# Starting every weight slab on a whole 256 bytes in a convolution and gated-FFN kernel on TensorE

## The chip, the core and the metric

The kernel runs on one core of one Trainium2 chip. The metric is device time in microseconds (us) of one execution. The kernel before takes 1324.0 us, the median of three runs (1322.94 to 1324.1).

The engines carry the names of the profile: PE is TensorE's matmuls, PEld its weight loads (they run beside the matmuls), DVE is VectorE, ACT is ScalarE, POOL is GpSimd, SP is SyncE, which here only issues DMAs. SBUF is the on-chip memory that the tiles lie in: 128 partitions, and in each a line of bytes. An address below is a byte in that line, the same in every partition.

## The reference

The first half is a short dynamic convolution: for each token and each of 8 heads, a softmax over 7 weights mixes the token with its 6 predecessors. The second is a gated feed-forward layer.

```python
w = exp(weight_gen - max);  w = w / (sum(w) + 1e-9)        # (4, 4096, 8, 7)
out[b,s,h,:] = sum_k w[b,s,h,k] * x_pad[b, s+k, h, :]       # x: (4, 4096, 192)
x = out.reshape(16384, 192)
gate = 1 / (1 + exp(-(x @ w_gate)))                         # w_gate: (192, 1536)
val  = x @ w_val                                            # w_val:  (192, 1536)
y    = (gate * val) @ w_out                                 # w_out:  (1536, 192)
```

## The kernel before

**Work and tiles.** The 16384 tokens are cut into 33 blocks: two of 256 tokens, then 31 of 512. The 1536 hidden features are cut into 12 slices of 128, numbered f = 0 to 11. One block with one slice is a *period*; there are 33 x 12 = 396 of them, and TensorE runs them one after the other.

**Weights.** Each slice f has one weight *slab* that stays in SBUF for the whole run: a tile of 128 partitions x 1152 fp32 numbers, 4608 bytes in each partition. It holds the gate, value and output weights of the slice twice, as a high and a low part, so that products of two parts each give more precision (`convert`; the split is made once, at the start). The slab is first the landing place of the raw weights (`raw`), and becomes `W` in place. Slabs 10 and 11 are used once more before that, for selection matrices (`sel_h`, `sel_t`), and so they are the first two that are allocated.

**Matmuls.** All matmuls of the periods come from line 911, in `emit`. Each uses 64 of TensorE's 128 rows: its weights are 64 partitions x 128 columns of a slab, its moving operand 64 partitions x 512 tokens (256 in the first two blocks) of `A`, `As` or `T` (the convolved tokens, in two parts) or of `hh` and `hl` (gate times value, in two parts). Two such matmuls, one on the lower and one on the upper 64 rows, run side by side; the text calls this a *pair*, and the time from the start of one matmul to the start of the next on the same 64 rows the *pitch*. A period has 14 pairs: 18 matmuls with slab f (gate and value), 10 with the slab of an earlier period, three periods back from block 4 on (the output product). In a block, therefore, the periods of f = 10 and 11 load 18 of their 28 weights from slab 10 or 11, those of f = 1 and 2 load 10 of 28 from them, and f = 0, which lies between, none; f = 3 to 9 use slabs 0 to 9 alone.

**The other engines.** DVE convolves the next block (lines 688 and 734), and for each period multiplies gate and value (L970) and forms `hl` (L976). ACT makes the sigmoid (L967) and `hh` (L973). After the last slice of a block, ACT moves the head of the output out of PSUM (L1023); by the three-period delay this stands right behind the period of f = 2. POOL does nothing but a 1 x 1 memset of the tile `seen` (L906), which passes the turn when one output bank goes from the upper to the lower rows. `w2` holds the softmax of the very first block (128 partitions x 7 x 32 numbers); it is used at the start only. `eye` is a small matrix for `convert`.

**Order.** A planner in the program (`Plan.order`) simulates the engines with fixed costs and so decides the order of all instructions. No address of a tile enters into it.

**Addresses.** Tiles of the pool `sb` are laid out in the order in which they are first asked for, each beginning on a multiple of 32 bytes. All tiles from `w0` to `cu1` end on a multiple of 256 bytes. Then come `w2` (896 bytes), `eye` (1024), slabs 11 and 10, `seen` (4 bytes, so 32 with the gap), and slabs 0 to 9. The moving operands `A`, `As`, `T`, `hh` and `hl` all begin on a multiple of 256; inside a slab every group of 128 columns begins a multiple of 256 bytes behind the slab's start.

Of the kernel before, what the change touches and what calls it, by code (L numbers as in the profile page):

```python
# [9 lines left out]
F32 = mybir.dt.float32  # L10
F32R = mybir.dt.float32r
# [219 lines left out]
def conv_gated_ffn(ctx: ExitStack, tc: tile.TileContext, xt, wg, wcat, outT):  # L231
# [13 lines left out]
    P = 128  # L245
    B, D, SP_ = xt.shape
    NF = wcat.shape[0]
    H, K = 8, 7
# [13 lines left out]
    sb = ctx.enter_context(tc.tile_pool(name="sb", bufs=1))  # L262
# [71 lines left out]
    t = 20.0  # L334
# [248 lines left out]


    CH = blks[0][2] // 8
    w2 = sb.tile([P, K, CH], F32R, name="w2")
    ident = plan.places["ev"][0]["buf"][:, :P]
    eye = sb.tile([P, 2, P], F32R, name="eye")

# [299 lines left out]


    writer = {}
    seen = sb.tile([1, 1], F32, name="seen")
    SYNC = mybir.DependencyInfo(mybir.DependencyClass.Sync, mybir.DependencyReason.DATA)

    def emit(slots):
# [234 lines left out]
```

## Time and profile before

| what | value |
|---|---|
| median of three runs | 1324.0 us (1322.94 to 1324.1) |
| the profiled execution's own time | 1323.46 us |
| its span, first to last instruction | 1321.7 us |
| PE busy | 1294.5 us, 98% |
| PEld busy | 1218.1 us, 92% |
| DVE busy | 1019.4 us, 77% |
| ACT busy | 619.7 us, 47% |
| POOL busy | 136.0 us, 10% |
| granted TensorE clock | 0.999 of full speed |
| chain that ended last: PE | 94% |

Busy time is the time in which an engine ran at least one instruction, so two matmuls side by side count once, and a busy PE is not by itself a PE at its peak. The chain that ended last is followed back from the last instruction, at each step to what released it. PE makes up nearly all of it, and the granted clock is full almost everywhere.

### The profile page before, as it was taken

What the parts mean: (1) busy time and instruction counts of PE and PEld (TensorE: products, weight loads), DVE (VectorE), ACT (ScalarE), POOL (GpSimd) and SP (SyncE); (2) the same over time, 40 slices, a digit from 0 to 9 for tenths busy, and PEclk for the clock granted to TensorE, in tenths of its full rate; (3) what the DMA queues carried; (4) which work ended last, traced back from release to release, by engine and by line L of the source; (5) the groups of instructions that cost most, each with busy time, mean ns of one, the idle gap of its engine ahead of it and who ended that gap; (6) DMA issues with size and microseconds to landing.
All of it is one profiled execution on the core that took longest, in us unless ns stands there. A gap on an engine that the chain in (4) does not pass through costs nothing.

```text
span 1321.7 us, 29878 instructions
## 1 busy us (share of the span) xinstructions
PE 1294.5 (98%) x11196; PEld 1218.1 (92%) x11196; DVE 1019.4 (77%) x1522; ACT 619.7 (47%) x1090; POOL 136.0 (10%) x1517
## 2 busy tenths in 40 slices
PE   5989999999999999999999999999999999999998
PEld 3787888899999999999999998888899999999997
DVE  8989799979998998787766778766688776654443
ACT  5756554454445564444444444444444444444443
POOL 0111101111111111111111111111111111111110
PEclk9999999999999999999999999999999999999999
DMA  8472886459898645534544443544453441011100
GB/s 275 104 161 52 171 181 144 97 129 188 177 187 194 155 105 140 132 99 102 126 99 113 124 120 85 129 107 115 109 132 91 111 116 42 13 37 37 37 13 13
DMA packets 59233, 150.81 MB, mean 114 GB/s; under 512 B 12688, under 2 KB 30992, under 8 KB 59088
## 3 DMA queue, kind: packets, MB, share of 16 engines
q1 hardware_dynamic: 59088, 148.91, 47.1%
q8 instruction: 87, 1.43, 0.5%
q14 instruction: 58, 0.48, 0.1%
HBM read 110.66 MB, written 16.20 MB: 96 GB/s over the span
## 4 chain that ended last, share of the span: by engine, by line
PE 94%; DVE 2%; ACT 1%; issue 1%; DMA 0%; SPq 0%; ACTq 0%; DVEq 0%; POOL 0%; POOLq 0%
PE bank L911 93%; PE bank L448 1%; DVE prod L688 0%; DVE prod L734 0%; DVE sg L970 0%; DMA w<-in_weight_gen 0%; DVE prod L757 0%; PE bank L449 0%; DVE ce L419 0%; DVE hl L976 0%; PE bank L450 0%; DMA out<-osb 0%; DVE cr L432 0%; ACT As L803 0%; DVE acc L688 0%
## 5 line engine op out<-in xcount | busy, mean ns | idle before, releaser
L911 PE MATMUL bank<-hh,W 64*128 64x512 f32 (+1 forms) x2376 | 789.3, 387 | 0.7 <-POOL seen L906 0.3
L911 PE MATMUL bank<-As,W 64*128 64x512 f32 (+1 forms) x2376 | 667.6, 387 | 0.0
L911 PE MATMUL bank<-T,W 64*128 64x512 f32 (+1 forms) x2376 | 661.9, 385 | 0.5 <-ACT T L843 0.4
L911 PE MATMUL bank<-hl,W 64*128 64x512 f32 (+1 forms) x1584 | 607.2, 385 | 3.6 <-DVE hl L976 3.6
L911 PE MATMUL bank<-A,W 64*128 64x512 f32 (+1 forms) x2376 | 496.3, 386 | 1.3 <-DVE A L786 1.3
L973 ACT CAST hh<-sg 128x512 fp32r<-128x512 f32 (+1 forms) x396 | 240.7, 608 | 496.2 <-DVE sg L970 494.1
L911 PEld LDWEIGHTS bank<-hh,W 64*128 64x128 f32 x2376 | 432.9, 184 | 17.2 <-POOL seen L906 2.8
L911 PEld LDWEIGHTS bank<-As,W 64*128 64x128 f32 x2376 | 431.4, 184 | 13.6 <-issue 0.3
L911 PEld LDWEIGHTS bank<-T,W 64*128 64x128 f32 x2376 | 430.2, 184 | 14.2 <-ACT T L843 1.0
L970 DVE TENSOR_TENSOR sg<-bank,sg 128x512 f32<-128x512 f32 (+1 forms) x396 | 265.6, 671 | 187.6 <-PE bank L911 181.9
L976 DVE TENSOR_TENSOR hl<-sg,hh 128x512 fp32r<-128x512 f32 (+1 forms) x396 | 264.9, 669 | 95.0 <-ACT hh L973 92.5
L911 PEld LDWEIGHTS bank<-A,W 64*128 64x128 f32 x2376 | 321.3, 184 | 16.4 <-DVE A L786 1.6
L967 ACT ACTIVATE sg<-bank 128x512 f32<-128x512 f32 (+1 forms) x396 | 231.9, 586 | 170.2 <-PE bank L911 166.9
L911 PEld LDWEIGHTS bank<-hl,W 64*128 64x128 f32 x1584 | 291.3, 184 | 13.8 <-DVE hl L976 5.0
L906 POOL MEMSET seen<- 1x1 f32 x1511 | 135.3, 90 | 1178.9 <-PE bank L911 1174.4
L734 DVE TENSOR_TENSOR prod<-x,wb 128x1024 f32<-128x1024 f32 x126 | 135.8, 1079 | 0.1
L688 DVE TENSOR_TENSOR prod<-prod,prod 128x1024 f32<-128x1024 f32 (+1 forms) x97 | 107.6, 1109 | 0.0
L734 DVE TENSOR_TENSOR prod<-xt,wt 128x1024 f32<-128x1024 f32 (+1 forms) x64 | 68.5, 1071 | 0.8
L688 DVE TENSOR_TENSOR acc<-prod 128x512 f32<-128x512 f32 (+1 forms) x66 | 35.5, 539 | 0.8
L827 DVE TENSOR_TENSOR T<-acc,T 64x256 fp32r<-64x256 f32 (+1 forms) x66 | 26.9, 408 | 1.3 <-ACT T L824 0.3
L824 ACT CAST T<-acc 64x256 fp32r<-64x256 f32 (+1 forms) x66 | 26.2, 397 | 0.8
L1029 DVE TENSOR_TENSOR osb<-bank,ev 64x512 f32<-64x512 f32 (+1 forms) x33 | 21.8, 661 | 5.0 <-ACT ev L1026 4.9
(52 smaller groups left out, 370.7 us busy)
## 6 DMA issues: line engine op xcount, KB each, us to landing
wb<-ws SPq DMA_DIRECT2D x63, 896.0 KB
wt<-ws SPq DMA_DIRECT2D x63, 448.0 KB
As<-A SPq DMA_DIRECT2D x56, 256.0 KB
x<-in_x SPq DMA_DIRECT2D x31, 259.0 KB
out<-osb SPq DMA_DIRECT2D x31, 256.0 KB
T<-T SPq DMA_DIRECT2D x56, 128.0 KB
raw<-in_w SPq DMA_DIRECT2D x12, 576.0 KB
out<-osb SPq DMA_DIRECT2D x33, 128.0 KB
```

The costliest lines, as they stand in the source:

```text
L448: nc.tensor.matmul(dst, eye[:, 0].bitcast(F32), buf[E].bitcast(F32)[:, a:z], start=True, stop=False)
L688: nc.vector.tensor_tensor(out=dst(buf), in0=a(buf), in1=b(buf), op=ALU.add)
L734: nc.vector.tensor_tensor(out=dst.rearrange("p (k i t) -> p k i t", k=z - k, t=M), in0=sliding(buf[X][:, k : k + cols], z - k, [[M, cols / ...
L824: nc.scalar.copy(buf[T][rows, 0, own], buf[ACT_][rows, :M2])
L827: ENG[e].tensor_tensor(out=buf[T][rows, 1, own], in0=buf[ACT_][rows, :M2], in1=buf[T][rows, 0, own].bitcast(F32), op=ALU.subtract,)
L906: turn = nc.gpsimd.memset(seen, 0.0)
L911: ins = nc.tensor.matmul(buf[dst][:, :n], w, m[:, :n], start=start, stop=stop)
L967: nc.scalar.activation(out=buf[k["sg"]][:, :N], in_=buf[k["g"]][:, :N], func=AF.Sigmoid)
L970: nc.vector.tensor_tensor(out=buf[k["sg"]][:, :N], in0=buf[k["v"]][:, :N], in1=buf[k["sg"]][:, :N], op=ALU.mult)
L973: nc.scalar.copy(buf[k["hh"]][:, :N], buf[k["sg"]][:, :N])
L976: ENG[e].tensor_tensor(out=buf[k["hl"]][:, :N], in0=buf[k["sg"]][:, :N], in1=buf[k["hh"]][:, :N].bitcast(F32), op=ALU.subtract)
L1029: nc.vector.tensor_tensor(out=buf[OT][LOW, :N], in0=buf[PT][LOW, :N], in1=buf[EV][LOW, :N], op=ALU.add)
```

## The change

Two small tiles are made larger; only the part that was there before is used.

```diff
-    w2 = sb.tile([P, K, CH], F32R, name="w2")
+    w2 = sb.tile([P, 320], F32R, name="w2")[:, : K * CH].rearrange("p (k t) -> p k t", k=K)
...
-    seen = sb.tile([1, 1], F32, name="seen")
+    seen = sb.tile([1, 128], F32, name="seen")[:, :1]
```

`w2` grows from 896 to 1280 bytes in each partition and `seen` from 4 to 512. What lies behind them in SBUF moves up. The start addresses in the built programs, with the rest by 256 in brackets:

```
tile         before          after
w2           168448 (0)      168448 (0)
eye          169344 (128)    169728 (0)
slab 11      170368 (128)    170752 (0)
slab 10      174976 (128)    175360 (0)
seen         179584 (128)    179968 (0)
slab 0       179616 (160)    180480 (0)
slab 1       184224 (160)    185088 (0)
...
slab 9       221088 (160)    221952 (0)
```

The instructions of all five engines stand in the same order in both programs, with the same shapes; the places in memory alone differ. Before, slabs 10 and 11 begin 128 bytes behind a multiple of 256, and slabs 0 to 9 begin 160 bytes behind one.

## Rows read from the trace of the kernel before

**Rows 1.** The page, busy time of TensorE: us, share, instructions.

```profile
PE 1294.5 (98%) x11196; PEld 1218.1 (92%) x11196; DVE 1019.4 (77%) x1522; ACT 619.7 (47%) x1090; POOL 136.0 (10%) x1517
```

**Rows 2.** Windows: stretch and length, PE, PEld, DVE, ACT, POOL busy; clock; DMA.

```profile
0.00:33.00 33.00, 17.09 (x86) 12.79 (x88) 28.77 (x63) 18.46 (x42) 0.71 (x6) 1.00 0.85 276
33.00:66.00 33.00, 31.59 (x296) 25.44 (x294) 30.91 (x64) 24.24 (x60) 4.09 (x32) 1.00 0.42 104
...
264.00:528.00 264.00, 264.00 (x2267) 261.09 (x2265) 236.80 (x349) 132.27 (x214) 27.70 (x312) 1.00 0.71 160
...
792.00:1056.00 264.00, 264.00 (x2268) 237.41 (x2266) 196.93 (x279) 114.82 (x197) 27.39 (x309) 1.00 0.45 111
...
1280.00:1321.00 41.00, 36.10 (x295) 33.79 (x291) 15.60 (x23) 14.52 (x24) 3.52 (x40) 0.96 0.07 20
```

**Rows 3.** Waits of PE: who waited for whom, us in total, times, longest.

```profile
PE bank L622 <- ACT w L559: 8.2, 1, 8.2
PE bank L449 <- ACT W L439: 5.1, 2, 3.8
PE bank L911 <- DVE hl L976: 3.6, 5, 1.2
```

**Rows 4.** Groups by line and shape, matmuls: count, busy us, mean ns.

```profile
L911 PE MATMUL bank<-hh,W 64*128 64x512 f32 x2232 | 754.8, 392 | 0.3 <-POOL seen L906 0.3
...
L911 PE MATMUL bank<-hl,W 64*128 64x512 f32 x1488 | 581.4, 392 | 0.9 <-DVE hl L976 0.9
```

**Rows 5.** Timeline of PE in a period of f = 6, upper rows: start, us.

```profile
1135.20 0.39 PE L911 MATMUL bank<-hl,W 64*128 64x512 f32 x1
...
1135.43 0.39 PE L911 MATMUL bank<-hh,W 64*128 64x512 f32 x1
...
1135.67 0.40 PE L911 MATMUL bank<-hl,W 64*128 64x512 f32 x1
...
1135.90 0.39 PE L911 MATMUL bank<-A,W 64*128 64x512 f32 x1
```

**Rows 6.** Timeline of ACT, the output's way out of PSUM, two blocks running.

```profile
1124.29 0.59 ACT L1023 COPY osb<-bank 128x512 f32<-128x512 f32 x1
...
1163.48 0.59 ACT L1023 COPY osb<-bank 128x512 f32<-128x512 f32 x1
```

**Rows 7.** Windows over f = 3 to 9, then 10 to 2, twice.

```profile
1124.47:1147.34 22.87, 22.87 (x200) 22.87 (x197) 17.02 (x23) 9.53 (x16) 2.40 (x27) 1.00 0.06 18
1147.34:1163.66 16.32, 16.32 (x144) 16.32 (x142) 11.98 (x19) 7.40 (x14) 1.68 (x19) 1.00 0.20 49
1163.66:1186.54 22.88, 22.88 (x200) 22.88 (x198) 11.20 (x17) 9.53 (x16) 2.40 (x27) 1.00 0.06 19
1186.54:1202.84 16.30, 16.30 (x144) 16.30 (x142) 8.61 (x14) 7.47 (x14) 1.68 (x19) 1.00 0.20 50
```

**Rows 8.** Timeline of PE in a period of f = 10, lower rows, four starts, all from slab 10.

```profile
1148.36 0.39 PE L911 MATMUL bank<-As,W 64*128 64x512 f32 x1
...
1149.06 0.40 PE L911 MATMUL bank<-T,W 64*128 64x512 f32 x1
```

**Rows 9.** Groups of weight loads in one period of f = 10 (1147.34 to 1150.59).

```profile
L911 PEld LDWEIGHTS bank<-As,W 64*128 64x128 f32 x6 | 1.1, 184 | 0.0
...
L911 PEld LDWEIGHTS bank<-A,W 64*128 64x128 f32 x7 | 1.1, 184 | 0.0
```

**Rows 10.** Groups of weight loads over the whole run, output product.

```profile
L911 PEld LDWEIGHTS bank<-hh,W 64*128 64x128 f32 x2376 | 432.9, 184 | 17.2 <-POOL seen L906 2.8 <-issue 1.0
```

**Rows 11.** Timeline of PE in a block of 256 tokens, upper rows, four starts.

```profile
87.40 0.27 PE L911 MATMUL bank<-hh,W 64*128 64x256 f32 x1
...
87.75 0.28 PE L911 MATMUL bank<-hl,W 64*128 64x256 f32 x1
```

**Rows 12.** Windows while raw weights land: slab 9, then slab 10.

```profile
23.07:24.47 1.40, 1.14 (x3) 0.79 (x4) 1.34 (x5) 1.32 (x4) 0.00 (x0) 1.00 1.03 425
24.47:25.87 1.40, 1.40 (x6) 0.92 (x6) 1.40 (x3) 1.34 (x5) 0.00 (x0) 1.00 1.02 421
```

## The prediction

> **What bounds the kernel now.** I read the busy times first: PE is busy for 98% of the span [rows 1]. A busy share alone proves little, so the windows come next. In the first 33 us PE works 17.09 us, and the next 33 us still have a small gap; from then on PE fills its stretches, 264.00 of 264.00 us, at the full granted clock [rows 2]. PE's waits say the same from the other side: the three longest sums, 8.2, 5.1 and 3.6 us, are waits for the first weights and the first values [rows 3]; they are over before the blocks of 512 tokens set in.
>
> So the question is what sets the pace of a matmul, since nobody makes PE wait. The matmuls over 512 tokens are the bulk: the two rows of the output product alone count 2232 and 1488 [rows 4], and by the structure of 14 pairs in each of 31 x 12 periods there are 5208 pairs. On one half of the rows the starts are 1135.20, .43, .67 and .90, so three pitches take 0.70 us, 0.2333 each [rows 5]. The output leaves PSUM once in a block, at 1124.29 and again at 1163.48, 39.19 us apart [rows 6]; divided by 12 x 14 pairs that is 0.2333 again. Thirty-one such blocks make 1215 us of the span of 1321.7. DVE is busy 236.80 us in one stretch of 264 and 196.93 in another, DMA 0.71 and 0.45, and the number of matmuls is 2267 and 2268 [rows 2]. The pace is PE's own: it does not depend on what the other engines or the DMAs do. PEld shows one thing more: it is busy for 261.09 us in the first of these stretches and for 237.41 in the second. Loads on the two halves overlap more in one than in the other, and the pace is the same. How the loads of the two halves lie to each other does not set it.
>
> **The change, part by part.** No instruction is added, removed or moved, on any engine or queue, and no wait. What could cost or gain is the access to the moved tiles: weight loads from the slabs (each of the 11088 matmuls of line 911 has one), the DMAs and the ACT and DVE instructions that fill the slabs at the start, `eye` and `w2` at the start, and the memset of `seen`.
>
> Weight loads. The trace holds its own comparison: slabs 10 and 11 begin at 128 by 256, a multiple of 64 bytes; slabs 0 to 9 begin at 160, which is none. In a period of f = 10, where 18 of 28 loads come from slab 10, the loads take 184 ns in the mean [rows 9]; over the whole run, where ten slabs of twelve lie at 160, they take 184 ns [rows 10]. The load itself does not see the difference.
>
> The pace. Seven periods of f = 3 to 9, all at 160, take 22.87 and 22.88 us, 3.268 each. The five periods f = 10, 11, 0, 1, 2, in which 56 of 140 loads are at 128, take 16.32 and 16.30 us, 3.264 and 3.260 each [rows 7]. (The counts in these rows contain four matmuls that reach over the borders.) Five periods at the other pace would be 16.34, so the mixed ones are 0.02 to 0.04 us shorter in a block, at the limit of what these windows resolve. If aligned loads earn that, it grows with their number; if it belongs to the change of alignment between neighbouring loads, it goes away when all are alike, and 31 blocks cost 0.6 to 1.2 us. I take the second, because inside a run of nine loads from slab 10 on one half three pitches, from 1148.36 to 1149.06, are again 0.70 us [rows 8]. I charge +0.5 us, the low end, as the windows resolve no more.
>
> What stands in the trace nowhere is a slab at a whole 256, where its low address bits equal those of the moving operands. From above the cost is bounded by the longest pitch that [rows 5] show, 0.24 us: if every pitch were that, 5208 x 0.0067 = +35 us. From below by the shortest, 0.23: 5208 x 0.0033 = -17 us. The nearest row is the pair at 128 against 160, with nothing beyond a few hundredths in 16 us, so I take 0 and keep both ends for the range.
>
> There is one more reason for 0. Over 256 tokens the first of four starts on the upper rows is at 87.40 and the last at 87.75, so a pitch is 0.117 us [rows 11], half of 0.2333. The same load of 128 columns stands before half as many columns there. If a badly placed load cost a fixed time in each pitch, the short pitch would be more than half of the long one, 0.117 against 0.1167. It is not, so no fixed part is visible for an alignment to take away. The reservation is that at 256 tokens the load could itself be the bound and hide that.
>
> The Trainium skill (TensorE: Matmul & The Clock Gate, section Back-to-back issue gap) puts a warm matmul over 512 columns at about 215.7 ns from start to start, and says that in streams of loads and matmuls both set the spacing. Here 233.3 ns are measured, 17.6 more; were all of it due to misplaced loads, 5208 x 17.6 ns = 92 us would be to be had by that page. The proportion of the two pitches speaks against it, and the sum takes nothing from it.
>
> The start. Twelve raw slabs land there. While slab 9 (at 160) lands, the DMAs move 425 GB/s, and 421 while slab 10 (at 128) does, over 1.40 us each [rows 12]. So placing gains nothing here: 0 us. Even 5% of twelve such landings would be 0.8 us, and PE's first wait of 8.2 us is for ACT [rows 3].
> The Trainium skill (DMA: Bandwidth & Descriptors, section How a descriptor splits into AXI transactions) says that a transaction begins on a 256-byte boundary and that bytes fetched ahead of an unaligned start cost time. By it 4608 bytes from 160 would take 149 beats of 32 bytes instead of 144, 3.5% of 12 x 1.40 us, or 0.6 us less in the sum; it speaks of what is read, and the equal rates show no such cost for these writes.
>
> `seen` is one element on POOL, busy 136.0 us in all [rows 1], and the matmuls of `hh` wait 0.3 us for it in the whole run [rows 4]; `w2` and `eye` are read in the first stretch only. Nothing for these.
>
> Sum, against the profiled execution's own time of 1323.46 us (span 1321.7 and 1.8 around it, 0.5 under the median of the runs): 1323.46 + 0.5 = 1323.9 us.
>
> **The rivals.**
> *Aligned loads earn.* The 0.02 to 0.04 us that a block saves with 56 aligned loads grows to all 336, six times as much: 0.12 to 0.24 us in each of 31 blocks, 4 to 7 us. For it: the sign in both blocks of [rows 7]. Against: 184 ns in [rows 9, 10] alike. Time: about 1318 us.
> *The long pitch goes.* Of three pitches in [rows 5] one is 0.24 and two are 0.23; if the long one comes from loads that straddle a boundary and vanishes, -17 us, 1306 us. For it: an uneven pitch in an undisturbed engine wants a cause. Against: the same 0.70 with slab 10 [rows 8].
> *Loads and moving operands collide.* This is the slower side. All moving operands begin at a multiple of 256; after the change all weights do too, where they now lie 128 or 160 bytes off. If a load and a matmul that starts with it then reach for the same part of the memory, the pitch goes towards 0.24. It decides as soon as it costs 0.5 ns in a pitch (2.6 us); a third of the bound of 35 us, +12 us, is my price: 1336 us. For it: nothing of this kind was ever in the trace. Against: 128 and 160 should differ too, were such distances decisive.
> *The change does not do what it says* is excluded by the addresses of the built program.
>
> **How the numbers follow.** Forecast as summed: 0.60, with its own range of 1321.5 to 1326. Aligned loads earn: 0.16. The long pitch goes: 0.09, of which 0.03 is for a gain beyond its 17 us. Collision: 0.15, most of it small, 1327 to 1332. From 1311 to 1330 lie the first two and part of each of the others, a little over 0.8. About 0.2%, 2.6 us, is what a measurement of this kernel can tell from no change; so faster 0.25, same 0.60, slower 0.15.
>
> **What would show it.** Right: three pitches of one half again 0.70 us; blocks 39.19 to 39.20 us apart at L1023; periods of f = 10 to 2 no shorter than the others; loads of 184 ns; PE's waits as before, all at the start. Wrong: any other distance of the L1023 rows. 0.1 us in it is 3 us in the time, and the rows of weight loads and of starts on one half would then say whether the load or the matmul behind it changed.

## The result, and the profile after

The changed kernel takes 1290.26 us, the median of four runs (1289.87 to 1291.78), against 1324.05 us: a ratio of 0.9749, with a 95% interval of 0.9732 to 0.9766. That is 2.5% or 33.8 us faster, far outside the range of 1311 to 1330 that the prediction gave. The profiled execution has a span of 1288.1 us.

The page of the kernel after, its busy times (us, share, instructions); they answer to [rows 1]:

```profile
PE 1261.3 (98%) x11196; PEld 1041.8 (81%) x11196; DVE 1014.9 (79%) x1522; ACT 608.7 (47%) x1090; POOL 135.8 (11%) x1517
```

PE has shed 33.2 us, which is nearly the whole gain. PEld has shed 176 us, though the number of loads is the same; we come to that. PE's waits have hardly changed. The same three groups as in [rows 3], of the kernel after (who waited for whom, us in total, times, longest):

```profile
PE bank L622 <- ACT w L559: 7.8, 1, 7.8
PE bank L449 <- ACT W L439: 5.0, 2, 3.8
PE bank L911 <- DVE hl L976: 3.7, 5, 1.2
```

So no wait went away. PE itself became quicker, with full occupation in both. The windows of the kernel after (stretch and length, then PE, PEld, DVE, ACT and POOL busy, clock, DMA share and GB/s), first two of those in [rows 2], then the two kinds of period of [rows 7]:

```profile
264.00:528.00 264.00, 264.00 (x2332) 218.21 (x2330) 242.52 (x362) 132.67 (x219) 28.28 (x318) 1.00 0.71 164
792.00:1056.00 264.00, 264.00 (x2334) 218.18 (x2332) 199.87 (x284) 113.96 (x201) 28.34 (x320) 1.00 0.47 116
...
1058.20:1080.41 22.21, 22.21 (x199) 18.36 (x196) 17.30 (x24) 9.35 (x16) 2.39 (x27) 1.00 0.25 65
1080.41:1096.28 15.87, 15.87 (x144) 13.12 (x141) 11.61 (x18) 7.14 (x14) 1.68 (x19) 1.00 0.20 51
```

In the same 264 us there are now 2332 and 2334 matmuls where there were 2267 and 2268. A period of f = 3 to 9 takes 22.21 / 7 = 3.173 us, one of the other five 15.87 / 5 = 3.174: all twelve are alike, 3% shorter than the 3.268 us of before. The output leaves PSUM at these times (ACT in the kernel after, the rows that answer to [rows 6]):

```profile
1096.14 0.58 ACT L1023 COPY osb<-bank 128x512 f32<-128x512 f32 x1
...
1134.22 0.58 ACT L1023 COPY osb<-bank 128x512 f32<-128x512 f32 x1
```

A block is now 38.08 us instead of 39.19, 1.11 us less, and 31 blocks make 34.4 us. That accounts for the whole gain of 33.8 us. Some of the first of these blocks gain less (blocks 2, 4 and 5: 0.42, 0.92 and 0.78 us), which covers the 0.6 us that this is too much; why they do was not followed up. The pitch can be seen in the timeline of PE (start, us), one stretch in a period of f = 5, where the two halves of the rows stream `hh` or `hl` and `As` or `T`:

```profile
1066.58 0.39 PE L911 MATMUL bank<-As,W 64*128 64x512 f32 x1
1066.58 0.39 PE L911 MATMUL bank<-hh,W 64*128 64x512 f32 x1
1066.81 0.39 PE L911 MATMUL bank<-As,W 64*128 64x512 f32 x1
1066.81 0.39 PE L911 MATMUL bank<-hh,W 64*128 64x512 f32 x1
...
1067.26 0.39 PE L911 MATMUL bank<-T,W 64*128 64x512 f32 x1
1067.26 0.39 PE L911 MATMUL bank<-hh,W 64*128 64x512 f32 x1
```

Three pitches, 1066.58 to 1067.26, take 0.68 us against 0.70 in [rows 5]: 0.2267 each. The two halves also start in the same hundredth of a microsecond, where before they stood 0.09 and 0.14 apart: between the starts of the upper rows at 1135.20 and 1135.43 in [rows 5] stands this one of the lower rows.

```profile
1135.29 0.40 PE L911 MATMUL bank<-As,W 64*128 64x512 f32 x1
```

Halves in step have their loads beside each other, so PEld can be busy for less time without a single load being shorter; a kernel below (all at 64) shows this apart from the pitch. The loads of the output product, against 184 ns in [rows 10], in the kernel after:

```profile
L911 PEld LDWEIGHTS bank<-hh,W 64*128 64x128 f32 x2376 | 433.1, 184 | 47.5 <-POOL seen L906 2.8 <-issue 1.0
```

And over 256 tokens nothing has moved: four starts on the upper rows, from 86.24 to 86.59, are three pitches of 0.117 us, as in [rows 11].

```profile
86.24 0.28 PE L911 MATMUL bank<-hh,W 64*128 64x256 f32 x1
...
86.59 0.28 PE L911 MATMUL bank<-hl,W 64*128 64x256 f32 x1
```

So the gain is 6.7 ns in each pitch of a matmul over 512 columns. The place of the weights is all that changed, and yet the load shows the same duration.

### The profile page after: what moved, and what is told of

Read it like the earlier page. It is cut to its first block, busy times and chain, and to the rows that moved or that the text cites. A ratio compares the mean times of both kernels' runs of the same rounds, so it can differ in the third digit from the quotient of the medians.

```text
span 1288.1 us, 29878 instructions
## 1 busy us (share of the span) xinstructions
PE 1261.3 (98%) x11196; PEld 1041.8 (81%) x11196; DVE 1014.9 (79%) x1522; ACT 608.7 (47%) x1090; POOL 135.8 (11%) x1517
## 4 chain that ended last, share of the span: by engine, by line
PE 95%; DVE 3%; ACT 1%; issue 1%; DMA 0%; SPq 0%; ACTq 0%; DVEq 0%; POOL 0%; POOLq 0%
PE bank L911 93%; PE bank L448 1%; DVE prod L688 0%; DVE prod L734 0%; DVE sg L970 0%; DMA raw<-in_w 0%; DVE prod L757 0%; DVE hl L976 0%; PE bank L449 0%; DVE ce L419 0%; PE bank L450 0%; DVE cr L432 0%; ACT As L803 0%; ACT ce L401 0%; DVE ce L407 0%
## 5 line engine op out<-in xcount | busy, mean ns | idle before, releaser
L911 PE MATMUL bank<-hh,W 64*128 64x512 f32 (+1 forms) x2376 | 776.3, 381 | 0.7 <-POOL seen L906 0.3
L911 PE MATMUL bank<-As,W 64*128 64x512 f32 (+1 forms) x2376 | 653.8, 382 | 0.0
L911 PE MATMUL bank<-T,W 64*128 64x512 f32 (+1 forms) x2376 | 648.4, 380 | 0.6 <-ACT T L843 0.4
L911 PE MATMUL bank<-hl,W 64*128 64x512 f32 (+1 forms) x1584 | 599.3, 380 | 3.7 <-DVE hl L976 3.7
L911 PE MATMUL bank<-A,W 64*128 64x512 f32 (+1 forms) x2376 | 477.9, 381 | 1.3 <-DVE A L786 1.3
L911 PEld LDWEIGHTS bank<-A,W 64*128 64x128 f32 x2376 | 291.5, 184 | 47.3 <-DVE A L786 1.6
```

The costliest lines, as they stand in the source:

```text
L911: ins = nc.tensor.matmul(buf[dst][:, :n], w, m[:, :n], start=start, stop=stop)
```

## The experiments

In all of them the plan and the order of the instructions are those of the kernel before; only places in memory differ.

**Which start of the slabs is short.** Four kernels set the slabs to other remainders by 256, through the sizes of `w2` and `seen`.

```diff
  (w2 alone)      w2 [P, 320], seen as before     slabs 10, 11 at 0, slabs 0 to 9 at 32
  (seen alone)    w2 as before, seen [1, 128]     all slabs at 128
  (all at 64)     w2 [P, 336], seen [1, 128]
  (all at 160)    w2 [P, 360], seen [1, 128]
```

> The growth of w2 alone: slabs 10 and 11 begin at 0 by 256, slabs 0 to 9 at 32. Theory 256 (only a start on a whole 256 bytes gives the short pitch): some 1322 to 1324 us, pitch 0.233 us where f = 3 to 9. Theory 64 (a start on a whole 64 bytes is enough): the same, 1322 to 1324, since 32 is no multiple of 64. Theory mixture (the long pitch comes from neighbouring loads with different starts): 1324. It tells which of the two edits carries the gain, and whether slabs 10 and 11 at 0 earn anything while the others do not.

Measured: 1320.44 us, ratio 0.9974 (0.9962 to 0.9985). The growth of `w2` alone earns a tenth of the change.

> The growth of seen alone: all twelve slabs begin at 128 by 256. Theory 256: as before, 1322 to 1326 us, pitch 0.233. Theory 64: as after the change, 1290 us, pitch 0.2267. Theory mixture: 1290 us too, as all loads are alike.

Measured: 1319.64 us, ratio 0.9982 (0.9963 to 1.0001). The five runs fall into two groups, three at 1318.67 to 1319.64 and two at 1323.49 and 1323.55, so the median says little here. Neither edit alone does it.

> Both tiles larger, w2 by 64 bytes more than in the change: all slabs begin at 64 by 256. Theory 256: 1322 to 1326 us. Theory 64: 1290 us. Theory 128 (a whole 128 bytes is wanted): 1322 to 1326. Theory mixture: 1290.

Measured: 1324.09 us, ratio 1.0000 (0.9989 to 1.0011).

> Both tiles larger, w2 by 160 bytes more than in the change: all twelve slabs begin at 160 by 256, where ten of them were before. Theory 256 and theory 64: 1324 us, pitch 0.2333 in all periods. Theory mixture: 1290 us, since no load differs from its neighbours any more.

Measured: 1323.90 us, ratio 1.0002 (0.9990 to 1.0013).

Theory mixture falls with the last three, theory 64 with the second and third, and theory 128 with the second, where all slabs begin on a whole 128. Of the theories written down 256 is left. The kernel at 64 answers one more question. Its busy times, then its timeline of PE, in a period:

```profile
PE 1294.8 (98%) x11196; PEld 1046.2 (79%) x11196; DVE 1019.4 (77%) x1522; ACT 617.7 (47%) x1090; POOL 137.1 (10%) x1517
...
825.19 0.40 PE L911 MATMUL bank<-hh,W 64*128 64x512 f32 x1
825.19 0.40 PE L911 MATMUL bank<-As,W 64*128 64x512 f32 x1
...
825.89 0.39 PE L911 MATMUL bank<-hh,W 64*128 64x512 f32 x1
825.89 0.39 PE L911 MATMUL bank<-T,W 64*128 64x512 f32 x1
```

Here too the halves start together, and three pitches are 0.70 us. That the halves run in step is not what makes them quick. It does go with the short busy time of PEld: 1046.2 us here, with the long pitch, and 1041.8 us after the change, with the short one.

**Whole 256, or 256 apart.** In the kernel after the moving operands begin on a whole 256 as well. These kernels move them, by unused bytes ahead of `A` (all the tiles behind move along, and `w2` is sized to put the slabs where they are wanted).

```diff
+    sb.tile([P, 32], F32, name="pad")          # 128 bytes; 16 numbers for 64 bytes
     for t in ("A", "As", "T"):
         place(t, 2, [P, 2, N], F32R)
...
  (moving at 128, slabs at 0)    w2 [P, 288], seen [1, 128]
  (both at 128)                  w2 [P, 320], seen [1, 128]
  (both at 64, 64 bytes ahead)   w2 [P, 320], seen [1, 128]
  (slabs at a whole 512)         w2 [P, 384], seen [1, 128], no bytes ahead
```

> All slabs at a whole 256 as after the change, but 128 unused bytes ahead of A move the moving operands A, As, T, hh and hl to 128 by 256. Theory own start (a load is short when its own weights begin on a whole 256, wherever the moving operand lies): 1290 us. Theory distance (weights and moving operand must lie a multiple of 256 apart): about 1320 us, as when the slabs alone were at 128. Theory all operands (each operand that begins off 256 costs by itself): over 1290, some 1300 to 1325.

Measured: 1324.26 us, ratio 0.9994 (0.9979 to 1.0009). Two of the eight runs are at 1319.28 and 1319.80 and six at 1323.82 to 1325.62, the same two groups as with the slabs alone at 128. What puts a run into one or the other was not found; neither is near 1290. The slabs lie as in the changed kernel, and the gain is gone.

> Moving operands and all slabs at 128 by 256, so that they lie a multiple of 256 apart, as after the change, while neither begins on a whole 256. Theory own start: 1320 us, as with the slabs alone at 128. Theory distance: 1290. Theory all operands: 1320 or more.

Measured: 1291.36 us, ratio 0.9759 (0.9731 to 0.9787). No slab begins on a whole 256, and the gain is there.

> w2 larger by 256 bytes more than in the change: all slabs begin on a whole 512 (and still a whole 256), the moving operands 256 bytes behind one. Theory own start with a boundary at 256: 1290 us, no difference to the change. Theory boundary at 512 or more: 1270 or lower. Theory distance counted by 512: slower than 1290.

Measured: 1289.98 us, ratio 0.9749 (0.9720 to 0.9777).

> Moving operands and all slabs at 64 by 256. Theory own start: 1324 us, as with the slabs alone at 64. Theory distance: 1290. Theory all operands: 1324 or more.

Measured: 1290.30 us, ratio 0.9751 (0.9723 to 0.9779).

Theories own start and all operands fall, distance counted by 512 falls too, and so does the description of the change as a matter of whole 256 bytes. What counts is the distance between the weights and the moving operands: a multiple of 256 is short, in all four places that were tried. The blocks show it without the noise of whole runs: ACT moving the output out, first where the moving operands alone are at 128, then where both are.

```profile
1125.49 0.59 ACT L1024 COPY osb<-bank 128x512 f32<-128x512 f32 x1
...
1164.69 0.59 ACT L1024 COPY osb<-bank 128x512 f32<-128x512 f32 x1
```

```profile
1096.42 0.58 ACT L1024 COPY osb<-bank 128x512 f32<-128x512 f32 x1
...
1134.51 0.58 ACT L1024 COPY osb<-bank 128x512 f32<-128x512 f32 x1
```

39.20 us a block in the first, 38.09 in the second.

**How the cost goes with the distance.** Distance is from here on the start of the weights less that of the moving operand, by 256. This kernel and the three behind it were run once each, with one run of the kernel before beside them. From block 4 on a period loads from slab f and slab f-3 alone, so that slabs with the same remainder of f by 3 can have a distance of their own, and one run shows three.

```diff
+    where, at = {}, [128]
     def slab(f, what, dtype):
-        return sb.tile([P, 2 * CT], dtype, name=f"{what}_{f}", tag=f"slab_{f}")
+        if f not in where:
+            where[f] = ((32, 96, 192)[f % 3] - at[0]) % 256
+            at[0] += (where[f] + 8 * CT + 31) // 32 * 32
+        t = sb.tile([P, 2 * CT + where[f] // 4], dtype, name=f"{what}_{f}", tag=f"slab_{f}")
+        return t[:, where[f] // 4 :]
...
  (w2 as before, seen [1, 128])
```

> Each slab stands some bytes into a larger tile, so that slabs 0, 3, 6, 9 begin at 32, slabs 1, 4, 7, 10 at 96 and slabs 2, 5, 8, 11 at 192 by 256, the moving operands at 0. From block 4 on a period loads from slab f and slab f-3 alone, so each period has one distance. Theory distance, only 0 is short: all three kinds of period take 3.25 to 3.27 us, total 1318 to 1324 us. Theory nearness (the cost grows with the distance to the nearest multiple of 256): 32 shorter than 96, 192 like 64 (3.267).

Measured: 1318.62 us, against 1323.39. The first matmul of each of four periods, f = 3, 4, 5 and 6, on PE (start, length; a row can hold several matmuls):

```profile
808.11 0.63 PE L917 MATMUL bank<-A,W 64*128 64x512 f32 x3
...
811.38 0.69 PE L917 MATMUL bank<-A,W 64*128 64x512 f32 x4
...
814.66 0.62 PE L917 MATMUL bank<-A,W 64*128 64x512 f32 x3
...
817.87 0.63 PE L917 MATMUL bank<-A,W 64*128 64x512 f32 x3
```

From start to start: 3.27 us at 32, 3.28 at 96, 3.21 at 192.

> As the kernel with 32, 96 and 192, with slabs 0, 3, 6, 9 at 16, slabs 1, 4, 7, 10 at 224 and slabs 2, 5, 8, 11 at 240 by 256. Theory distance, only 0 is short: 3.25 to 3.27 us in all. Theory nearness: 16 and 240 near 3.173 us, 224 like 32. If the best distance is a little off 0, one of them is under 3.173.

Measured: 1304.37 us, against 1323.39. The same four starts:

```profile
800.04 0.61 PE L917 MATMUL bank<-A,W 64*128 64x512 f32 x3
...
803.22 0.63 PE L917 MATMUL bank<-A,W 64*128 64x512 f32 x3
...
806.49 0.63 PE L917 MATMUL bank<-A,W 64*128 64x512 f32 x3
...
809.68 0.61 PE L917 MATMUL bank<-A,W 64*128 64x512 f32 x3
```

3.18 us at 16, 3.27 at 224, 3.19 at 240. So the cost is not a matter of 0 alone: 16 bytes off cost 0.01 us in a period at most, which the passage from the period before may account for, 32 bytes cost all of it, and 192 less than half (0 gives 3.174, and 3.27 is the full cost). Theory nearness explains 16 and 240, but not 32 against 192. Nothing is shorter than 0, so nothing that was run beats the changed kernel; the kernels at a whole 512 and with both at 64 equal it.

**Which half is slowed.** A load brings weights into one half of the rows while a matmul streams on that half and another on the other. Two kernels mix distances.

```diff
  (hh and hl at 64)     w2 [P, 304], seen [1, 128]
+    sb.tile([P, 16], F32, name="pad")
     place("hh", 4, [P, N], F32R)
...
  (slabs at 0 and 64)   as the kernel with 32, 96 and 192, with
+            where[f] = ((0, 64)[f // 3 % 2] - at[0]) % 256
```

> All slabs at a whole 256 and A, As and T too; only hh and hl, the moving operands of the output product, begin at 64 by 256. In 5 of 14 pairs of a period one of the two halves then streams hh or hl (2 to 6 on the upper rows, 9 to 13 on the lower), so in 10 of 14 pairs one half is off. Theory own half (a load is disturbed by the matmul that streams on its own 64 rows): in a half the pitches beside hh and hl are 0.233 and the others 0.2267; 10 of 28 matmuls, period 3.173 + 10/28 x 0.093 = 3.21 us if the halves are free of each other, 1302 us. Theory both halves (a load is disturbed by what the other half streams too): up to 10 of 14 pairs, 3.24 us, 1313 us.

Measured: 1303.76 us, against 1323.39. The total is near that of theory own half, and so is the place. PE's timeline in a stretch where the lower rows stream `hh` and `hl` (at 64) and the upper ones `As` and `T` (at 0), all loads being at 0:

```profile
804.63 0.39 PE L912 MATMUL bank<-hh,W 64*128 64x512 f32 x1
804.67 0.39 PE L912 MATMUL bank<-As,W 64*128 64x512 f32 x1
...
805.57 0.39 PE L912 MATMUL bank<-hl,W 64*128 64x512 f32 x1
805.58 0.39 PE L912 MATMUL bank<-T,W 64*128 64x512 f32 x1
```

Between the first and the last lie four pitches on each half: 0.94 us for `hh` and `hl`, 0.235 each, and 0.91 for `As` and `T`, 0.2275 each. I put all starts of the trace to the two halves by the order of their operands, from block 5 on: 232.2 ns where a half streams `hh` or `hl`, 226.7 to 228.8 where it streams the others.

The price is another matter. The theory charged `hh` and `hl` the full cost; but weights at 0 and moving operands at 64 are at distance 192, and there the kernel with 32, 96 and 192 lost only 3.21 - 3.174, some 0.04 us in a period, with all 28 matmuls at it. Here 10 of 28 cost as much: 3.21 us a period again. So the distance on a matmul's own half does not fix the cost by itself. One thing differs between the two: in the kernel with 192 the halves stand 0.06 us apart, as these two starts in a period at 192 show, here 0.01 to 0.04.

```profile
816.73 0.39 PE L917 MATMUL bank<-hh,W 64*128 64x512 f32 x1
816.79 0.39 PE L917 MATMUL bank<-As,W 64*128 64x512 f32 x1
```

Whether that is the reason was not tested. At 160 such a difference costs nothing: the kernel before, where the halves drift, and all at 160, where they start within 0.01 us of each other, take 1323.86 and 1323.90 us. So "192 less than half" holds for that one kernel.

> All moving operands at 0; slabs 0 to 2 and 6 to 8 begin at 0, slabs 3 to 5 and 9 to 11 at 64 by 256. From block 4 on a period loads its gate and value weights from the one kind and its output weights from the other, so in 10 of 14 pairs one half loads at distance 0 and the other at 64. Theory own half (a load that is off lengthens the pitch on its own 64 rows): on a half the pitch is 0.2267 where its loads are at 0 and 0.2333 where they are at 64; half of the loads, 3.22 us in the mean of the periods, about 1307 us. Theory other half (a load that is off lengthens the pitch of the half beside it): the long pitches stand beside the loads at 64, on the half whose loads are at 0; the same total. Theory any (one load that is off is enough for both halves): 12 of 14 pairs long in the mean, 3.25 us, 1319 us.

Measured: 1312.46 us, against 1323.40: between theory own half and theory any. Sorted in the same way, the mean pitch is 228.8 to 229.4 ns on a half whose load is at 0 and 232.8 to 233.5 where it is at 64, as one counts the load of the matmul that streams or that of the next. The half that loads from 64 bears the larger part, but the other is not free of it. So theory other half falls with both kernels; whether the remainder is an effect of what the half beside it reads, or comes from the two halves sharing one stream of instructions, stays open.

## Why the prediction was wrong

**The bound was read rightly.** The pace of TensorE alone set the time, and 5208 pairs carried the gain: 5208 x 6.67 ns = 34.7 us. No other engine took its place, and PE's waits are within half a microsecond of what they were. (One wait for `hl`, 0.9 us in [rows 4], does fall to matmuls over 512 tokens, against what the prediction reads from [rows 3]; nothing hangs on it.)

**The step that failed** is the one on the place that stands nowhere in the trace: "The nearest row is the pair at 128 against 160, with nothing beyond a few hundredths in 16 us, so I take 0". That term of the sum, put at 0, was about -34 us. The comparison was sound for what it compared: all slabs at 128 and all at 160 differ by 0 to 5 us, as the runs at 128 fall (ratios to before 0.9982 and 1.0002, with intervals that overlap). But both are on the dear side. I read the addresses as "a multiple of 64, or none", and the trace had no load near the distance that matters. Two nearly equal points showed that the cost hardly differs between them, not that there is none. The other term, +0.5 us for a gain from changing alignment that would be lost, was not there either: all at 160 takes 1323.90 us, the kernel before 1323.86 beside it.

**The bound from below was no bound.** I took the shorter of the pitches in [rows 5], 0.23, as the least a pitch could become, which gave -17 us. The starts are printed to 0.01 us, so an even 0.2333 reads as 0.23 and 0.24 as well, and both stand for one distance only. The mean pitch moved to 0.2267, twice as far.

**The reason from 256 tokens did not hold.** I argued that 0.117 is half of 0.2333, so that no cost of a fixed size per load is visible. After the change the short pitch is still 0.117 and the long one 0.2267, less than twice as long. So the proportion of one half is no rule. The reservation, that the load itself may bound the pitch over 256 tokens, fits, but was not tested.

**The equal 184 ns misled.** The load has the same duration in the records at either distance, in both kernels; the pitch of the matmuls pays. That a load's own duration stays the same did not show what it does to its neighbours. The Trainium skill (TensorE: Matmul & The Clock Gate, section Step-by-step: what each phase is for) has the load and the streaming operand on read ports of their own, and says: "Loading the next tile's weights doesn't steal SBUF read bandwidth from the running matmul." This case does not bear that out: with the distance alone changed, a pitch of 233.3 ns became 226.7, and it was mainly the half that streamed at a distance from its loads that was slow. That the two reads are what meets is an inference; no run shows it directly.

**The rivals.** The collision had the right variable, the distance of weights and moving operands, with the sign turned round: the pitch was long at 128 and 160, and short at 0. "Aligned loads earn" had the right sign and a sixth of the size, by luck: all slabs at 64 are as aligned as it asks for, and take 1324.09 us. The 0.02 to 0.04 us in [rows 7] may come from the loads at 128, where some runs gain 4 to 5 us and others nothing. "The long pitch goes" had the sign and half of the size, for a reason that falls too: with both at 64 no load begins on a whole 256, and 1290.30 us is as quick. The remark that 17.6 ns would be to be had pointed the right way: 6.7 of them came, and 11 are left. Its 215.7 ns is, by the Trainium skill (TensorE: Matmul & The Clock Gate, section Back-to-back issue gap), the gap of a matmul by itself, not the spacing in a stream of loads and matmuls. No run here comes down to it, and whether the 11 can be had is open.

**The start.** Costing the raw slabs' landing at nothing was not tested by itself; PE's first waits are 7.8 and 5.0 us, against 8.2 and 5.1, and the first matmul over 512 tokens starts at 95.53 us, against 95.81. That 0.3 us does not follow the place: it starts at 95.56 with all slabs at 160, and at 96.81 with the slabs at a whole 256 and the moving operands at 128.

What stays open is the mechanism: why distances of 16 and 240 cost little, 32, 64, 96, 128, 160 and 224 nearly all, and 192 a part in one kernel and more in another. The reads of a load and of a stream meeting in the same part of the memory fits the half that is slowed, but no run here shows the memory's parts.

## What to carry to other kernels

Where TensorE never waits, look at where its two operands lie, and try weights and moving operands a multiple of 256 bytes apart in a partition. In this kernel it cost under 900 bytes in a partition, and one tile of odd size ahead of the weights was enough to lose it. It was shown for matmuls of 64 rows over 512 columns, each with a load of its own; over 256 columns it gained nothing. When a trace offers two points that agree, ask whether both lie on the same side of what you change.

## What the runs showed that I had not expected

- Places in memory alone were worth 2.5%, with the same instructions in the same order: 6.7 ns in the pitch of each 512-column matmul on 64 rows.
- The two halves of the rows drift against each other: 0.09 and 0.14 us apart in the kernel before, together in the kernel after, with full occupation in both. PEld's busy share, 92% and 81%, goes with this drift and not with the pitch: all at 64 has 79% and the long pitch.
- With weights and moving operands 128 apart, the runs of two kernels fall into two groups, about 1319 and about 1324 us; the eight runs each with all slabs at 64 and at 160, and the ten runs of four kernels at a distance of 0 (1289.42 to 1292.56), show no such gap.
